# A leftover tile's first-layer sums turned by VectorE and a trip through DRAM instead of by TensorE

## The chip, the cores and the metric

One core of a Trainium2 chip runs the kernel. The metric is the device time of one execution in microseconds (us). Before the change the median of three runs is 629.51 us (629.24 to 629.6). TensorE multiplies matrices, VectorE, ScalarE and GpSimd work elementwise, and SP and ScalarE issue the DMAs of this kernel. In the rows of the profile they are PE (PEld for its weight loads), DVE, ACT, POOL and SP; ACTq and SPq are the sequencers that issue DMAs.

## The reference

Windowed attention feeds a mixture of four experts with fixed weights (the first MLP), and that feeds a second MLP with h * cos(h) between its layers.

```python
def _moe_ref(x, domain_probs, w1, w2):          # x: 1152 x 512, four experts, F = 1024
    p = domain_probs / (domain_probs.sum(-1, keepdims=True) + 1e-09)
    for e in range(E):
        h = np.maximum(x @ w1[e], 0.0)
        out += p[:, e:e + 1] * (h @ w2[e])

def _moe2_ref(x, w_in, w_out):                  # 512 -> 2048 -> 512
    h = x @ w_in
    g = h * np.cos(h)
    return g @ w_out
```

## The kernel before

The 1152 tokens are nine tiles of 128: eight that are worked on as two blocks of 512 columns, and one leftover, tile 0. Every float32 product is three matmuls, over a first part in a shorter form (fp32r) and the rest (`PASSES`). The hidden columns are worked on in twelve groups of 512: groups 0 to 7 are the first MLP (`g < NG1`), 8 to 11 the second. A group has two phases.

In the products phase the eight tiles' first layer is computed by a scheme that needs seven products instead of eight. `pair(g, j)` (line 835) does one half of the group's columns: seven products of six matmuls each, into four PSUM banks `pa`, `pb`, `pc`, `pd`. VectorE forms sums between them: `u1 = pb + p1`, `c22 = pc + u1`, `c22 += pd`. The sixth product adds into `pc` and the seventh into `pd`, so they can't start before VectorE has read those banks for `c22`. In the second MLP (`early == 2`) the order is pa, pb, again pa, pc, pd, then the sixth (on pc) and the seventh (on pd). `finish` (line 753) makes the hidden values: Relu in the first MLP, a cosine chain in the second. `cosine` (line 704) is ScalarE read and round, a VectorE subtract (line 713), ScalarE sine, a VectorE multiply (line 722); `cosine_parts` splits the result in a first part (ScalarE) and a second part (GpSimd).

In the layer 2 phase, nine tiles of twelve matmuls each (`layer2`, line 937) go to `acc`. Tile 0 is placed where `"0"` or 0 stands. Somewhere in it `left(g + 1)` ("La", "Lb", line 795) computes the leftover's first layer of the next group, twelve matmuls, with tokens in the rows of PSUM. The second layer needs them with hidden columns in the rows: `turn_rows` ("X", line 821) transposes the four 128x128 blocks on TensorE, and ScalarE and VectorE split them into `h0`. In the first MLP Relu comes ahead of that (line 810), in the second the cosine (`cosine_rows`, line 734).

The order of the work is written by hand. `steps` (line 1020) lists each group's steps, and `run` (line 1096) does for each: the step's matmuls, `stages` advances of the open cosine chains, `njobs` pieces of weight preparation for the next group (a ScalarE copy and a GpSimd subtraction each, with the raw loads on SP), `ncv` pieces of weight conversion (groups 0 to 5: int64 words to float32 by ScalarE and VectorE, through DRAM), and then what follows the step's matmuls. Each engine works in the order of issue. In the second MLP `early_kind` is 2 for groups 9 to 11, and the second piece group of a group's weights (`second`, line 246) is done at the second and third product (`more`).

Group 8 and group 0 have places of their own for the leftover's turn (lines 1035 and 1166).

Of the kernel before, what the change touches and what calls it, by code (L numbers as in the profile page):

```python
# [10 lines left out]
F32 = mybir.dt.float32  # L11
# [4 lines left out]
AF = mybir.ActivationFunctionType  # L16
ALU = mybir.AluOpType
# [15 lines left out]
G = 512  # L33
NFG = G // 128
NG1, NG2 = E * F1 // G, F2 // G
NTT = NT // 128
MAGIC = 12582912.0
INV2PI = 0.15915494309189535
# [14 lines left out]
def tile_kernel(ctx, tc, qT, kT, v, probs, w_1, w_2, w_in, w_out, out):  # L53
    nc = tc.nc
# [3 lines left out]
    dram = pool("dram", bufs=1, space=DRAM)  # L58
# [8 lines left out]
    txp = pool("txp", bufs=4)  # L67
# [114 lines left out]

    wi32 = dram.tile([DM, F2], F32, name="wi32")
    wo32 = dram.tile([F2, DM], F32, name="wo32")

    def sub(eng, out, a, b):
        eng.tensor_tensor(out=out, in0=a, in1=b, op=ALU.subtract)  # L187
# [506 lines left out]
    h0 = hp.tile([128, 2, NFG, 128], F32R, name="h0")  # L694
# [9 lines left out]
    def cosine(ps, out):  # L704

        u = csp.tile([128, NB], F32, name="u", tag="c")
        r = csp.tile([128, NB], F32, name="r", tag="c")

        nc.scalar.activation(out=u, in_=ps, func=AF.Copy, scale=INV2PI, bias=0.25)
        nc.scalar.activation(out=r, in_=u, func=AF.Copy, bias=MAGIC)  # L710
        yield False
        yield False
        nc.vector.scalar_tensor_tensor(  # L713
            out=u, in0=r, scalar=MAGIC, in1=u, op0=ALU.subtract, op1=ALU.subtract
        )
        yield False
        nc.scalar.activation(out=u, in_=u, func=AF.Sin, scale=-TWOPI)
        yield False
        yield False
        if out is None:  # L720
            out = u
        nc.vector.tensor_tensor(out=out, in0=ps, in1=u, op=ALU.mult)
        yield out

    def cosine_parts(ps, hi, lo, eng):

        for u in cosine(ps, None):
            yield False
        nc.scalar.activation(out=hi, in_=u, func=AF.Copy)  # L729
        if eng is nc.vector:  # L730
            yield False
        sub(eng, lo, u, hi.bitcast(F32))

    def cosine_rows(ps, out):

        for _ in cosine(ps, out):
            yield False

    def chain(c, ch):
        next(ch)  # L740
        chains.append((c, ch))
# [48 lines left out]
    def sums():  # L790
        return bank([128, 512], "o_ps")

    rows_t = {}

    def left(g):

        ps = sums()
        for d in range(ND):
            for a, bb in PASSES:
                nc.tensor.matmul(  # L800
                    ps.rearrange("p (j f) -> p j f", j=2), x0[:, bb, d, :],
                    w1[:, :, a, 0, d * 256 : (d + 1) * 256],
                    start=(d == 0 and (a, bb) == PASSES[0]),
                    stop=(d == ND - 1 and (a, bb) == PASSES[-1]),
                )
            if d % 2:
                yield
        r = rows_t[g] = lp.tile([128, 512], F32, name="lt", tag="lt")
        if g < NG1:
            nc.scalar.activation(out=r, in_=ps, func=AF.Relu)  # L810
        else:
            chain(0, cosine_rows(ps, r))

    def half(step, end):

        next(step)
        yield
        if end:
            whole(step)

    def turn_rows(g):

        apart = mm is None
        assert not any(c == 0 for c, _ in chains)
        r = rows_t.pop(g)
        tp = bank([128, NFG, 128], "l_ps")
        for f in range(NFG):
            nc.tensor.transpose(tp[:, f, :], r[:, f * 128 : (f + 1) * 128], ident)  # L828
        yield
        nc.scalar.activation(out=h0[:, 0], in_=tp, func=AF.Copy)  # L830
        if apart:
            yield
        sub(nc.vector, h0[:, 1], tp, h0[:, 0].bitcast(F32))
# [86 lines left out]
    def ahead(g, t):  # L920

        opened[g, t] = sums()
        tile_matmuls(opened[g, t], g, t, range(NFG // 2))
        yield
# [12 lines left out]
    def layer2(g, t, ps=None):  # L937
        if (g, t) == (NG1 + NG2 - 1, LAST):
            yield from last_tile(g, t)
            return  # L940
        f0 = NFG // 2 if (g, t) in opened else 0
        ps = opened.pop((g, t), None) or ps or sums()
        tile_matmuls(ps, g, t, range(f0, NFG))
        yield
        o = acc(t)
        if g < NG1:
            s = pr[:, t, g // 2 : g // 2 + 1]
            if g == 0:
                nc.vector.tensor_scalar(out=o, in0=ps, scalar1=s, scalar2=None, op0=ALU.mult)
            else:  # L950
                nc.vector.scalar_tensor_tensor(  # L951
                    out=o, in0=ps, scalar=s, in1=o, op0=ALU.mult, op1=ALU.add
                )
        elif g == NG1:
            nc.vector.tensor_copy(o, ps)
        else:
            nc.vector.tensor_tensor(out=o, in0=ps, in1=o, op=ALU.add)  # L957
            if g == NG1 + NG2 - 1:
                store(t, o)
# [38 lines left out]
    def bank(shape, name):  # L998
        count[0] += 1
        from_, tag = ps1, "o_ps"  # L1000
        if mm is not None and count[0] % 4:
            from_, tag = mm[0]
            mm.append(mm.pop(0))
        return from_.tile(shape, F32, name=name, tag=tag)
# [15 lines left out]
    def steps(g):  # L1020

        last, turn = g == NG1 + NG2 - 1, g == NG1 - 1
        moe = g < NG1
        early_kind = 1 if g in (0, NG1) else 0 if moe else 2
        ps = [early.pop(j, None) or pair(g, j, early_kind) for j in range(2)]
        if g == 0:
            yield ahead(0, 0), 0, 0, 0
            for p in ps:  # L1030
                next(p)
            seq = [0, 1, 0, 1, 0, 0, 1, 0, "0", 1, 1]
            more = [1, 1, 0, 0, 0, 0, 0, 2, 1, 0, 0]
        elif g == NG1:
            seq = [0, 0, 0, 0, "X", 0, 1, 1, "0", 1, 1, 1]
            more = [0, 1, 1, 0, 0, 0, 0, 0, 0, 0, 0, 0]
        elif moe:
            seq = [0] * 7 + [1] * 7
            more = [0, 1, 1, 0, 0, 0, 0] + [0, 1, 1, 1, 1, 1, 1]
        else:  # L1040
            seq = [0] * 7 + ["0"] + [1] * 7
            more = [0, 1, 1, 0, 0, 0, 0, 0] + ([0] * 7 if last else [0, 1, 1, 0, 0, 0, 0])
        for j, m in zip(seq, more):
            if j == "X":
                yield turn_rows(g), 2, m, 0
            elif j == "0":
                yield layer2(g, 0), 2, m, 0
            else:
                yield ps[j], 1, m, 0
        nxt = None if last else left(g + 1)  # L1050
        ncv = {0: 2, 5: 3, 6: 3, 1: 3, "La": 3, 7: 3, 2: 3, 8: 3}
        if turn:
            order = (0, 1, "f0", 5, "f1", 2, "f5", 6, "f2", 3, "f6", 4, "f3", 7, "f4", 8, "f7")
            njobs = [2, 2, 0, 2, 0, 2]
        elif moe:
            order = (0, 5, 6, 1, "La", "Lb", 7, 2, 8, 3, "X", 4)
            njobs = [1] * 8
            if g == 0:
                order = (5, 6, 1, "La", "Lb", 7, 2, 8, 3, "X", 4)
                njobs[:3] = [2, 2, 2]  # L1060
                ncv = {5: 1, 6: 2, 1: 3, "La": 1, 7: 3, 2: 3, 8: 3}
        elif last:
            order, njobs = ("a5", "a6", "a7", "a8", "a1", 5, 6, 7, 8, 1, 2, 3, 4), []
        else:
            order = ("a5", "a6", "a7", "a8", "a1", "a2", 5, 6, 7, "La", 8, "Lb", 1, 2, 3, "X", 4)
            njobs = [0, 0, 0, 0, 0, 0, 1, 1, 1, 1, 1, 1, 1, 1, 1, 1, 2]
            if g == NG1:
                njobs[4:6] = [1, 1]
        for k, o in enumerate(order):
            m = njobs.pop(0) if njobs else 0  # L1070
            if isinstance(o, int):
                assert o == 0 or not any(c > 0 for c, _ in chains)
                yield layer2(g, o), 2, m, ncv.get(o, 0)
            elif o[0] == "f":
                yield flip(int(o[1])), 0, m, 0
            elif o[0] == "a":
                yield ahead(g, int(o[1])), 2 if last else 1, m, 0
            elif o[0] == "L":
                yield half(nxt, o == "Lb"), 2, m, ncv.get(o, 0)
            else:  # L1080
                yield turn_rows(g + 1), 2, m, 0
        if turn:
            yield from last_flip(g + 1, nxt)
# [24 lines left out]
    with tc.manual_schedule():  # L1108
# [19 lines left out]
        def leftover(end):  # L1128
            if not first:
                first.append(left(0))  # L1130
            return half(first[0], end)
# [146 lines left out]
```

## Time and profile before

| | |
|---|---|
| median of three runs | 629.51 us |
| span of the profiled execution, first to last instruction | 627.9 us |
| between the two (launch and end of a run) | 1.6 us |
| TensorE busy | 621.4 us, 99% |
| VectorE, ScalarE, GpSimd busy | 71%, 52%, 56% |
| granted TensorE clock | 0.999 |

The profiled execution has no time of its own beside its span, so sums are made against the span of 627.9 and carried to the runs by the 1.6 us. A group of the first MLP takes 46.7 us from one first product to the next (342.04 to 388.77), one of the second 46.7 or 46.8 (487.40 to 534.17). Times in the rows are us from the start of the span. A matmul's duration is its length in a pipeline; matmuls start closer together than that.

### The profile page before, as it was taken

The page shows a single profiled execution, that of the slowest core. Times are in us where ns is not written, and L with a number is a line of the kernel's source. Part 1 is how long each engine was busy: PE and PEld are TensorE (multiplying, and loading weights), DVE is VectorE, ACT ScalarE, POOL GpSimd, SP SyncE. Part 2 cuts the span into 40 slices and gives each one's busy share as a digit, 9 for nine tenths or more (in the row PEclk, how much of TensorE's full clock was granted, in tenths as well). Part 3 has the DMA queues.
Part 4 walks back from the last instruction along what each step waited for, and adds up shares of the span by engine and source line. Part 5 has one row for each costly group of instructions (what it writes and reads, how often), then busy time and mean ns, then how long its engine had stood idle before and what let it go on. Part 6 is the DMA issues. An engine that isn't in the chain of part 4 may idle for free.

```text
span 627.9 us, 9396 instructions
## 1 busy us (share of the span) xinstructions
PE 621.4 (99%) x3408; PEld 508.8 (81%) x3408; DVE 445.3 (71%) x776; ACT 324.0 (52%) x690; POOL 350.4 (56%) x338
## 2 busy tenths in 40 slices
PE   8999999999999999999999999999999999999997
PEld 6777888888888788888888888888788888888886
DVE  6878899589788788789689633656774664664663
ACT  6989444435444344344344331455883683673660
POOL 4868495463562482573553561592459479379340
PEclk9999999999999999999999999999999999999999
DMA  9651245147147147146143111120101201202003
GB/s 276 166 155 42 94 123 176 35 153 242 43 135 244 58 140 241 54 147 206 34 164 137 34 68 34 33 89 14 34 1 48 87 2 68 67 1 67 16 2 135
DMA packets 39118, 60.66 MB, mean 97 GB/s; under 512 B 4640, under 2 KB 21536, under 8 KB 39072
## 3 DMA queue, kind: packets, MB, share of 16 engines
q1 hardware_dynamic: 38528, 59.67, 29.6%
q8 instruction: 27, 0.44, 0.3%
q10 hardware_dynamic: 544, 0.39, 0.2%
q14 instruction: 19, 0.16, 0.1%
HBM read 49.30 MB, written 10.75 MB: 96 GB/s over the span
## 4 chain that ended last, share of the span: by engine, by line
PE 92%; DVE 3%; ACT 2%; POOL 1%; issue 1%; DMA 1%; SPq 0%; DVEq 0%; POOLq 0%
PE o_ps L930 46%; PE o_ps L771 33%; PE o_ps L800 5%; PE x_ps L612 2%; PE t_ps L576 1%; PE s_ps L506 1%; PE l_ps L828 1%; DMA wo<-cv 1%; PE r_ps L550 1%; PE o_ps L1114 1%; ACT p L525 1%; PE f_ps L984 1%; PE o_ps L968 0%; POOL w1t L187 0%; ACT r L710 0%
## 5 line engine op out<-in xcount | busy, mean ns | idle before, releaser
L930 PE MATMUL o_ps<-w2t,hpair 128*128 128x512 f32 x1140 | 267.4, 391 | 0.0
L930 PEld LDWEIGHTS o_ps<-w2t,hpair 128*128 128x128 f32 x1140 | 212.7, 188 | 43.8
L771 PE MATMUL o_ps<-xs,w1t 128*128 128x512 f32 x720 | 169.3, 390 | 0.0
L771 PEld LDWEIGHTS o_ps<-xs,w1t 128*128 128x128 f32 x720 | 134.6, 188 | 28.5 <-issue 0.4
L187 POOL TENSOR_TENSOR w2t<-raw,w2t 128x512 fp32r<-128x512 f32 x48 | 64.0, 1349 | 78.6 <-ACT w2t L211 78.4
L187 POOL TENSOR_TENSOR w1t<-raw,w1t 128x512 fp32r<-128x512 f32 x48 | 64.3, 1357 | 61.3 <-ACT w1t L211 60.2
L187 POOL TENSOR_TENSOR w1t<-sm,w1t 128x512 fp32r<-128x512 f32 x48 | 63.8, 1346 | 31.3 <-ACT w1t L211 31.0
L771 PE MATMUL o_ps<-xz,w1t 128*128 128x512 f32 x288 | 69.9, 390 | 0.4 <-DVE c L839 0.4
L187 POOL TENSOR_TENSOR hpair<-u,hpair 128x512 fp32r<-128x512 f32 x30 | 40.1, 1346 | 51.4 <-ACT hpair L729 51.4
L771 PEld LDWEIGHTS o_ps<-xz,w1t 128*128 128x128 f32 x288 | 53.7, 188 | 12.4 <-DVE c L839 1.0
L310 ACT ACTIVATE cr<-cr 128x512 f32<-128x512 f32 x32 | 21.7, 678 | 79.8 <-DVE cv L304 79.8
L951 DVE SCALAR_TENSOR_TENSOR accpair<-o_ps,pr,accpair 128x512 f32<-128x512 f32 x56 | 41.2, 745 | 27.0 <-PE o_ps L930 27.0
L757 ACT ACTIVATE hpair<-o_ps 128x512 fp32r<-128x512 f32 x47 | 28.1, 597 | 35.0 <-DVE o_ps L839 35.0
L748 DVE SCALAR_TENSOR_TENSOR hpair<-o_ps,hpair 128x512 fp32r<-128x512 f32 x47 | 32.3, 688 | 19.2 <-ACT hpair L757 19.1
L211 ACT ACTIVATE w1t<-sm 128x512 fp32r<-128x512 f32 x44 | 27.6, 628 | 31.9 <-POOL sm L187 31.7
L713 DVE SCALAR_TENSOR_TENSOR u<-r,u 128x512 f32<-128x512 f32 x36 | 28.1, 780 | 11.1 <-ACT r L710 11.0
L800 PE MATMUL o_ps<-w1t,x 128*128 128x512 f32 x144 | 35.7, 391 | 0.0
L957 DVE TENSOR_TENSOR accpair<-o_ps,accpair 128x512 f32<-128x512 f32 x23 | 15.7, 689 | 27.9 <-PE o_ps L930 27.9
L839 DVE TENSOR_TENSOR o_ps<-o_ps,u 128x512 f32<-128x512 f32 x48 | 33.3, 693 | 2.9 <-PE o_ps L771 2.6
L930 PE MATMUL o_ps<-w2t,h 128*128 128x512 f32 x144 | 35.2, 391 | 0.1
L304 DVE SCALAR_TENSOR_TENSOR cv<-cr,cv 128x512 int32<-128x512 int32 x32 | 33.6, 1050 | 1.1
L757 ACT ACTIVATE hpair<-c 128x512 fp32r<-128x512 f32 x17 | 10.7, 631 | 45.6 <-DVE c L839 45.6
(137 smaller groups left out, 873.8 us busy)
## 6 DMA issues: line engine op xcount, KB each, us to landing
raw<-w SPq DMA_DIRECT2D x32, 512.0 KB, 3.8
cr<-w_in SPq DMA_DIRECT2D x16, 512.0 KB, 4.3
cr<-w_out SPq DMA_DIRECT2D x16, 512.0 KB, 4.0
wi<-cv SPq DMA_DIRECT2D x16, 256.0 KB, 3.4
wo<-cv SPq DMA_DIRECT2D x16, 256.0 KB, 2.2
raw<-wi SPq DMA_DIRECT2D x8, 512.0 KB, 3.4
raw<-wo SPq DMA_DIRECT2D x8, 512.0 KB, 3.6
qt<-qT SPq DMA_DIRECT2D x8, 256.0 KB, 3.9
```

The lines of the kernel that those rows point to most:

```text
L187: eng.tensor_tensor(out=out, in0=a, in1=b, op=ALU.subtract)
L211: nc.scalar.activation(out=out, in_=src, func=AF.Copy)
L304: nc.vector.scalar_tensor_tensor(out=a, in0=hw, scalar=-0x40000000, in1=o, op0=ALU.bitwise_and, op1=ALU.bitwise_or,)
L310: nc.scalar.activation(out=fl(hw), in_=fl(hw), func=AF.Abs)
L713: nc.vector.scalar_tensor_tensor(out=u, in0=r, scalar=MAGIC, in1=u, op0=ALU.subtract, op1=ALU.subtract)
L748: nc.vector.scalar_tensor_tensor(out=out, in0=src, scalar=0.0, in1=hi.bitcast(F32), op0=ALU.max, op1=ALU.subtract)
L757: nc.scalar.activation(out=hi, in_=src, func=AF.Relu)
L771: nc.tensor.matmul(ps, w(a, k, m), operand_of_x(bb, b)[:, m], start=(start and m == 0 and (a, bb) == PASSES[0]), stop=(stop and m == 1 and ...
L800: nc.tensor.matmul(ps.rearrange("p (j f) -> p j f", j=2), x0[:, bb, d, :], w1[:, :, a, 0, d * 256 : (d + 1) * 256], start=(d == 0 and (a, ...
L839: add = lambda out, a, b: nc.vector.tensor_tensor(out=out, in0=a, in1=b, op=ALU.add)
L930: nc.tensor.matmul(ps, hidden(a, f, t), w_t[2, g, f // 2][:, bb, f % 2, :], start=(f == 0 and (a, bb) == PASSES[0]), stop=(f == NFG - 1 an ...
L951: nc.vector.scalar_tensor_tensor(out=o, in0=ps, scalar=s, in1=o, op0=ALU.mult, op1=ALU.add)
```

## The change

For all groups but 0 and 8 (`shuffled`), VectorE turns the 32x32 squares of the leftover's sums from PSUM into SBUF at the end of `left`. The sixteen squares' places within the 128x128 blocks are put right by DMA: `store_rows` writes them to a DRAM tensor with four stores (two from SP's queue, two from ScalarE's), issued ahead of tile 2 of layer 2, and `load_rows` fetches them with one load on SP, issued ahead of the step behind tile 2. No TensorE transpose remains for these groups. The split into `h0` moves to the next group's products phase: behind the fourth product in the first MLP. In the second MLP the cosine moves too: what is stored are the plain sums, and the cosine chain opens the products phase, advanced twice at each of the first three products. The one job that "X" had in the second MLP's list goes to tile 4.

```diff
-        nc.scalar.activation(out=u, in_=ps, func=AF.Copy, scale=INV2PI, bias=0.25)
+        like = (lambda t: t) if len(ps.shape) == 2 else (lambda t: t.rearrange("p (k t e) -> p k t e", k=NFG, e=32))
+        nc.scalar.activation(out=like(u), in_=ps, func=AF.Copy, scale=INV2PI, bias=0.25)
...
+    def shuffled(g):
+        return g not in (0, NG1)
+
+    def store_rows(g):
+        r = rows_t.pop(g)
+        to = rows32.rearrange("(q e) (t n) -> t e q n", e=32, t=4)
+        for t in range(4):
+            queue = nc.scalar if t % 2 else nc.sync
+            queue.dma_start(out=to[t], in_=r[32 * t : 32 * t + 32].rearrange("e (q n) -> e q n", q=4))
+
+    def load_rows(g):
+        r = rows_t[g] = txp.tile([128, 4, 128], F32, name="lm", tag="x1", bufs=1)
+        nc.sync.dma_start(out=r.rearrange("p t n -> p (t n)"), in_=rows32)
+
+    def shuffled_rows(g):
+        yield
+        src = rows_t.pop(g).rearrange("p t (k e) -> p k t e", e=32)
+        hi, lo = (h0[:, a].rearrange("p k n -> p (k n)") for a in range(2))
+        if g < NG1:
+            hi, lo = (x.rearrange("p (k t e) -> p k t e", k=NFG, e=32) for x in (hi, lo))
+            nc.scalar.activation(out=hi, in_=src, func=AF.Copy)
+            sub(nc.vector, lo, src, hi.bitcast(F32))
+        else:
+            chain(0, cosine_parts(src, hi, lo, nc.gpsimd))
...
         r = rows_t[g] = lp.tile([128, 512], F32, name="lt", tag="lt")
-        if g < NG1:
+        if shuffled(g):
+            if g < NG1:
+                nc.scalar.activation(out=ps, in_=ps, func=AF.Relu)
+            nc.vector.transpose(
+                r.rearrange("p (q k e) -> p q k e", q=4, e=32),
+                ps.rearrange("p (k q e) -> p q k e", q=4, e=32),
+            )
+        elif g < NG1:
...
         elif moe:
-            seq = [0] * 7 + [1] * 7
-            more = [0, 1, 1, 0, 0, 0, 0] + [0, 1, 1, 1, 1, 1, 1]
+            seq = [0] * 4 + ["X"] + [0] * 3 + [1] * 7
+            more = [0, 1, 1, 0, 0, 0, 0, 0] + [0, 1, 1, 1, 1, 1, 1]
         else:
-            seq = [0] * 7 + ["0"] + [1] * 7
-            more = [0, 1, 1, 0, 0, 0, 0, 0] + ([0] * 7 if last else [0, 1, 1, 0, 0, 0, 0])
-        for j, m in zip(seq, more):
+            seq = ["X"] + [0] * 7 + ["0"] + [1] * 7
+            more = [0, 0, 1, 1, 0, 0, 0, 0, 0] + ([0] * 7 if last else [0, 1, 1, 0, 0, 0, 0])
+        for k, (j, m) in enumerate(zip(seq, more)):
             if j == "X":
-                yield turn_rows(g), 2, m, 0
+                yield turn_rows(g), 0 if shuffled(g) else 2, m, 0
...
-                yield ps[j], 1, m, 0
+                yield ps[j], 2 if g > NG1 and k < 4 else 1, m, 0
...
-            order = (0, 5, 6, 1, "La", "Lb", 7, 2, 8, 3, "X", 4)
+            order = (0, 5, 6, 1, "La", "Lb", 7, 2, 8, 3, 4)
...
-            order = ("a5", "a6", "a7", "a8", "a1", "a2", 5, 6, 7, "La", 8, "Lb", 1, 2, 3, "X", 4)
-            njobs = [0, 0, 0, 0, 0, 0, 1, 1, 1, 1, 1, 1, 1, 1, 1, 1, 2]
+            order = ("a5", "a6", "a7", "a8", "a1", "a2", 5, 6, 7, "La", 8, "Lb", 1, 2, 3, 4)
+            njobs = [0, 0, 0, 0, 0, 0, 1, 1, 1, 1, 1, 1, 1, 1, 1, 3]
...
         for k, o in enumerate(order):
             m = njobs.pop(0) if njobs else 0
+            if nxt and shuffled(g + 1):
+                if o == 2:
+                    store_rows(g + 1)
+                if order[k - 1] == 2:
+                    load_rows(g + 1)
```

## Rows read from the trace of the kernel before

**Rows 1.** The page's part 1: busy us, share of the span, instructions.
```profile
span 627.9 us, 9396 instructions
...
PE 621.4 (99%) x3408; PEld 508.8 (81%) x3408; DVE 445.3 (71%) x776; ACT 324.0 (52%) x690; POOL 350.4 (56%) x338
```

**Rows 2.** The page's part 4: the chain that ended last, by engine.
```profile
PE 92%; DVE 3%; ACT 2%; POOL 1%; issue 1%; DMA 1%; SPq 0%; DVEq 0%; POOLq 0%
```

**Rows 3.** Timeline, start of group 10's products: start, us, engine, line, tiles [idle before].
```profile
532.79 2.55 POOL L187 TENSOR_TENSOR w2t<-raw,w2t 128x512 fp32r<-128x512 f32 x2 [0.24 <-ACT w2t L211]
...
534.17 6.96 PE L771 MATMUL o_ps<-xs,w1t 128*128 128x512 f32 x30
534.37 0.69 DVE L957 TENSOR_TENSOR accpair<-o_ps,accpair 128x512 f32<-128x512 f32 x1 [1.45 <-PE o_ps L930]
...
535.73 0.60 ACT L845 ACTIVATE p<-o_ps 128x512 f32<-128x512 f32 x1 [2.50 <-PE o_ps L771]
536.22 1.15 ACT L211 ACTIVATE w2t<-raw 128x512 fp32r<-128x512 f32 x2
536.92 2.54 POOL L187 TENSOR_TENSOR w2t<-raw,w2t 128x512 fp32r<-128x512 f32 x2 [1.58 <-ACT w2t L211]
537.16 0.69 DVE L839 TENSOR_TENSOR u<-o_ps,p 128x512 f32<-128x512 f32 x1 [2.10 <-PE o_ps L771]
538.45 0.60 ACT L709 ACTIVATE u<-o_ps 128x512 f32<-128x512 f32 x1 [1.08 <-PE o_ps L771]
...
539.81 0.69 DVE L839 TENSOR_TENSOR c<-o_ps,u 128x512 f32<-128x512 f32 x1 [1.96 <-PE o_ps L771]
540.42 0.68 DVE L713 SCALAR_TENSOR_TENSOR u<-r,u 128x512 f32<-128x512 f32 x1
...
540.97 2.88 PE L771 MATMUL o_ps<-xz,w1t 128*128 128x512 f32 x12
541.17 0.69 DVE L839 TENSOR_TENSOR c<-o_ps,c 128x512 f32<-128x512 f32 x1
```

**Rows 4.** Groups of instructions, shapes apart: count, busy us, mean ns, idle before.
```profile
L828 PE MATMUL l_ps<-ident,lt 128*128 128x128 f32 x48 | 7.2, 273 | 0.0
...
L955 DVE COPY accpair<-o_ps 128x512 f32<-128x512 f32 x8 | 5.4, 688 | 10.1 <-PE o_ps L930 10.1
```

**Rows 5.** Timeline of TensorE around one turn of the leftover, group 5.
```profile
338.85 0.60 PE L828 MATMUL l_ps<-ident,lt 128*128 128x128 f32 x4
339.21 2.99 PE L930 MATMUL o_ps<-w2t,hpair 128*128 128x512 f32 x12
342.04 6.96 PE L771 MATMUL o_ps<-xs,w1t 128*128 128x512 f32 x30
```

**Rows 6.** Timeline, group 10: GpSimd and VectorE at the same time.
```profile
547.13 1.30 POOL L187 TENSOR_TENSOR hpair<-u,hpair 128x512 fp32r<-128x512 f32 x1 [7.67 <-ACT hpair L729]
547.32 1.65 DVE L722 TENSOR_TENSOR u<-c,u 128x512 f32<-128x512 f32 x1
```

**Rows 7.** Timeline of ScalarE at the start: its queue issues two DMAs.
```profile
0.73 0.99 ACTq L168 DMA_DIRECT2D k<-kT  x2
```

**Rows 8.** Timeline, group 9: TensorE behind the leftover's last matmul.
```profile
525.52 5.61 PE L930 MATMUL o_ps<-w2t,hpair 128*128 128x512 f32 x24
```

**Rows 9.** DMA issues: count, KB each, median us from issue to landing.
```profile
vt<-v SPq DMA_DIRECT2D x8, 256.0 KB, 4.8
...
kt<-kT SPq DMA_DIRECT2D x3, 256.0 KB, 3.4
...
out<-acc SPq DMA_DIRECT2D x2, 128.0 KB, 2.3
```

**Rows 10.** Timeline of VectorE in the second pair of group 6.
```profile
355.84 0.69 DVE L839 TENSOR_TENSOR c<-o_ps,u 128x512 f32<-128x512 f32 x1 [0.60 <-PE o_ps L771]
```

**Rows 11.** Timeline of VectorE, then of TensorE, at group 3's products.
```profile
202.55 0.43 DVE L300 TENSOR_SCALAR cv<-cr 128x512 int32<-128x512 int32 x1 [1.81 <-DMA wo<-cv]
...
208.55 3.02 PE L771 MATMUL o_ps<-xz,w1t 128*128 128x512 f32 x12 [0.40 <-DVE c L839]
```

More of the change, by code (lines that the diff above doesn't have):

```diff
@@ L184, in tile_kernel @@
     wo32 = dram.tile([F2, DM], F32, name="wo32")
+    rows32 = dram.tile([128, G], F32, name="rows32")
     def sub(eng, out, a, b):
@@ L721, in cosine @@
             out = u
-        nc.vector.tensor_tensor(out=out, in0=ps, in1=u, op=ALU.mult)
+        nc.vector.tensor_tensor(out=like(out), in0=ps, in1=like(u), op=ALU.mult)
         yield out
@@ L821, in turn_rows @@
     def turn_rows(g):
+        if shuffled(g):
+            yield from shuffled_rows(g)
+            return
         apart = mm is None
@@ L1055, in steps @@
         elif moe:
-            order = (0, 5, 6, 1, "La", "Lb", 7, 2, 8, 3, "X", 4)
+            order = (0, 5, 6, 1, "La", "Lb", 7, 2, 8, 3, 4)
             njobs = [1] * 8
             if g == 0:
-                order = (5, 6, 1, "La", "Lb", 7, 2, 8, 3, "X", 4)
+                order = (5, 6, 1, "La", "Lb", 7, 2, 8, 3, 4)
                 njobs[:3] = [2, 2, 2]
```

## The prediction

> **What bounds the kernel now.** I read the page's busy table first, then TensorE's timeline around the step that goes, then the timeline of all engines in a second-MLP group, because the change adds its work there. TensorE is busy 99% of the span [rows 1], and the chain that ended last is 92% TensorE [rows 2]. So a matmul taken out is a gain, and any other engine matters only where TensorE has to wait for it. The reader should see how little waiting there is: 30 product matmuls take 6.80 us, from 534.17 to 540.97 [rows 3], so six take 1.36 and twelve 2.72.
>
> **The transposes that go.** Groups 1 to 7 and 9 to 11 lose four TensorE transposes each. The table of groups gives 273 ns for one [rows 4], which would make 40 x 0.273 = 10.9 us. That is a length in the pipeline, not a spacing. The block starts at 338.85, the next matmul at 339.21, and the next product at 342.04 [rows 5]: 3.19 us for the four transposes and twelve matmuls, and the twelve alone take 2.72. The step costs TensorE 0.47 us, so ten cost 4.7 us. It stands on the path, as TensorE waits for nothing before or behind it. This term is a gain for sure: **-4.7 us**.
>
> **What is added off TensorE.** VectorE turns 32x32 blocks out of PSUM. No row shows that operation. The nearest is the copy of the same size out of PSUM, 0.69 us [rows 4]; I take it, with 0.60 (ScalarE's read of a product, [rows 3]) and 1.65 (the longest VectorE row quoted, [rows 6]) as ends. The first MLP's Relu stays, in place. Then come four stores of 64 KB, two issued by SP and two by ScalarE, and a fetch of 256 KB on SP. Two issues on ScalarE's queue took 0.99 us [rows 7]. ScalarE's two issues wait for VectorE's turn, and what is queued behind them is weight copies that TensorE needs a group later; SP's fetch waits for the four landings, with raw weight loads (and, in groups 0 to 5, conversion traffic) behind it. I cost these queues at nothing on the path because the weights are a group ahead; the price if that cover is gone is the third rival.
>
> When does the fetch land? In groups 8 to 10 the leftover's last matmul ends at 525.52 in the group shown [rows 8]. Turn ends +0.9, the second issue is out at +1.3, a small store takes 2.3 [rows 9], so the fetch goes at about +3.7; 256 KB take 3.4 to 4.8 [rows 9], so it lands at +7.1 to +8.5. Between lie the rest of tile 1 and tile 2 (six matmuls each) and tiles 3 and 4 (twelve each): 1.36 + 1.36 + 2.72 + 2.72 = 8.16. It lands at about the first product of the next group, which I call P.
>
> **First MLP (groups 1 to 7).** The split of the leftover's hidden values moves between the products: one ScalarE operation (about 0.6) and one VectorE operation (0.69) after the fourth product. There VectorE is late by little: VectorE idles 0.60 us before the next pair's second sum at 355.84 [rows 10], so the shift is taken up. What wants care is the conversion groups. In group 3 TensorE already waits 0.40 us for VectorE's c sum, after VectorE waited 1.81 us for a conversion store to land [rows 11]. The turn adds 0.69 in front of that, the old subtraction (as long) goes behind it. So between -0.4 (the wait vanishes) and +0.7 (one turn's length added to it); I take **+0.15**.
>
> **Second MLP (groups 9 to 11), where I expect the gain to go.** The cosine of the leftover (read, round, VectorE subtract, sine, VectorE multiply, ScalarE first part, GpSimd second part) moves from the tiles of layer 2 to the first three products. Here is the order that the code gives, from P on, with times of [rows 3]. ScalarE operations of this size follow each other by 0.53 (two in 1.15), VectorE's by 0.61, GpSimd's by 1.27.
> - VectorE adds the last tile at +0.20, then the subtract of the cosine. GpSimd's two weight parts of layer 2 end at 535.34, P + 1.17, and P comes 0.47 earlier, so the subtract is done by +2.2 at the latest. ScalarE copies p1 at +1.56; the sine follows at +2.05 (+2.2 at the latest; what follows takes the early value), then the weight copy at +2.57 (it stood at +2.05). GpSimd's weight part begins at +3.27 and holds to +4.56.
> - VectorE's u1 sum is tied to TensorE at +2.99; the multiply is behind it, ready at +3.6. Both its inputs are in SBUF. A row shows what that costs: GpSimd works from 547.13 to 548.43, the same form of multiply starts at 547.32 and ends at 548.97 [rows 6], 0.54 after GpSimd. So it ends at +5.10 here.
> - ScalarE's first part +5.14, the second weight copy +5.67, and only then the read of product A, +6.19 (it stood at +4.28: 538.45), its rounding done at +7.44.
> - VectorE's subtract of that chain is queued ahead of the sum c += pd. GpSimd meanwhile does the leftover's second part (+5.84) and the second weight part (+7.09 to +8.38), so the subtract, ready at +7.48, ends at +8.92, and the sum at +9.55. It stood at 541.17, +7.00 [rows 3].
> - The seventh product adds into the bank that this sum reads, and is due at P + 8.16. It starts at +9.6: TensorE waits 1.44 us, plus about 0.1 for restarting (as behind the transposes, where twelve matmuls last 2.99 against 2.88 [rows 3, 5]): **1.55 us** in each of three groups, **+4.65**.
>
> Before, the margin at this place was 8.16 - 7.69 = 0.47 us. After the stall the chain is late by some 0.3 us against TensorE, which the next pair takes up.
>
> The Trainium skill (SBUF - State Buffer, Who interferes with whom) says that a VectorE instruction with two SBUF inputs fully blocks against a GpSimd one that reads SBUF, and that one with at most one SBUF input, outside the two-port modes, doesn't contend. The pair in [rows 6] agrees. By that rule the turns, which read PSUM, are exempt; if they were not, each could take up to 1.65, which the range holds.
>
> **Sum.** 627.9 (span) - 4.7 + 0.15 + 4.65 = 628.0. The runs' median lies 1.6 above the profiled span (629.51 against 627.9), so **629.6 us**: no change.
>
> **Rivals.** *A, the collision is half as bad or missing.* If GpSimd's weight part starts 0.35 us later than I placed it (0.15 of that is open above), so that the multiply gets the port first, the multiply ends at +4.28, the read of A starts at +5.36, and the subtract is ready at +6.66. If only that one meets GpSimd it ends near +8.1, the sum near +8.7, the wait is 0.65: -4.7 + 0.15 + 2.0 = 627.0. If neither does, 625.0. For it: a margin of 0.3 us between GpSimd's start and the multiply decides. Against: GpSimd has three parts back to back, and two tries to miss them.
> *B, the turn isn't what costs, and 10.9 us go.* The 273 ns would have to be a spacing; the next matmul starts 0.36 us after the first of four [rows 5]. 618.6 us, hardly.
> *C, the trip through DRAM is late.* ScalarE then stands at the cosine's first read with p1, the weight copies and A's read behind it, and TensorE waits for the sum of the fourth product as well. Up to about P + 2 the wait stays near 1.5, since the pieces then miss each other by other amounts. From there each us costs about one: a landing at P + 4 puts the multiply at +6.4, the first c sum at +7.05 against a product due at +6.80, the second at about +11: some 3.3 us a group, 9.9 in all, 634.9 us. For it: store and fetch cannot overlap, and raw weights of 512 KB share the queues. Against: by the rows it lands at about P, so it would need 2 us more than the slowest.
> The Trainium skill (VectorE: DVE Perf Modes, Rules for kernel authors) advises TensorE for 128x128 transposes whose result may go to PSUM, which is the old way; by that rule the new one loses, and C, or the collision above, is how it would do so here.
>
> **How the numbers follow.** This kernel's measurement can tell about 0.2%, 1.26 us, from no change; so "same" is 628.25 to 630.77. My forecast 0.42. Rival A 0.38 (625.0 to 628.2). B 0.01. C, and conversion groups losing more than 0.7 us, 0.19 (630.8 to 635). So faster 0.39, same 0.42, slower 0.19. The range leaves out one in ten at each end: 625.0 to 632.2; for the likeliest case alone it is 628.3 to 630.7.
>
> **What would show it.** Right: no transposes of l_ps in groups 1 to 7 and 9 to 11; the first MLP's seven groups each about 0.47 us shorter; in groups 9, 10 and 11 a gap on TensorE of 1 to 1.7 us ahead of the seventh product, put down to VectorE's c sum, and a multiply of about 1.5 us. Wrong: no gap there (A), or ScalarE idle at the cosine's first read until a DMA (C); VectorE turns far from 0.7 us; TensorE waiting for h0 at the leftover's tile; or gaps in groups 1 to 5, where conversion work is squeezed.

## The result, and the profile after

| | before | after |
|---|---|---|
| median | 629.38 us (629.22 to 629.6, 4 runs) | 633.88 us (633.35 to 635.06, 4 runs) |
| ratio after to before | | 1.0076, interval 1.0061 to 1.0091 |
| span of the profiled execution | 627.9 us | 633.1 us |
| TensorE busy | 621.4 us, 99% | 620.2 us, 98% |

The kernel became slower by 0.8%; I had said no change, 629.6 us, with 632.2 as the upper end. The page of after, part 1 (busy us, share, instructions) and the first line of part 4 (the chain that ended last), against [rows 1, 2]:

```profile
span 633.1 us, 9421 instructions
...
PE 620.2 (98%) x3368; PEld 505.9 (80%) x3368; DVE 453.8 (72%) x783; ACT 325.0 (51%) x690; POOL 352.7 (56%) x341
...
PE 87%; DVE 4%; ACT 3%; DMA 2%; issue 2%; POOL 1%; SPq 0%; DVEq 0%; POOLq 0%
```

TensorE has 40 instructions fewer, yet the chain is 87% TensorE instead of 92%: VectorE, ScalarE and DMAs have a larger part in it. To see where, I took the time from each group's first product to the next one's (the last group: to the last matmul). It is worked out from the start times of all product matmuls:

| group | 0 | 1 | 2 | 3 | 4 | 5 | 6 | 7 | 8 | 9 | 10 | 11 |
|---|---|---|---|---|---|---|---|---|---|---|---|---|
| before | 70.39 | 46.70 | 46.74 | 47.40 | 46.73 | 46.71 | 46.73 | 47.23 | 51.40 | 46.77 | 46.74 | 43.57 |
| after | 69.91 | 46.24 | 46.24 | 51.48 | 46.24 | 46.24 | 46.24 | 47.24 | 50.94 | 47.66 | 48.07 | 45.15 |

Seven groups lost 0.46 to 0.50 us: the transposes sit in the layer 2 phase of groups 0 to 6 and 8 to 10, one group ahead of their use. Group 3 gained 4.08, and groups 9, 10 and 11 gained 0.89, 1.33 and 1.58. With the 0.47 that groups 3, 9 and 10 also saved, group 3 lost 4.55 to waiting and the second MLP 4.74. Together -4.7 + 4.55 + 4.74 = 4.6 us; the median rose by 4.5. The span of the profiled execution rose by 5.2. This one was the longest of the four runs (635.06 us), and 0.5 of the 5.2 lies ahead of the first product, which starts between 36.7 and 38.3 us in the profiles of this document.

**Group 5, no transposes.** Timeline of TensorE in after where [rows 5] stood: layer 2 goes straight on to the next group's products.

```profile
337.84 6.51 PE L971 MATMUL o_ps<-w2t,hpair 128*128 128x512 f32 x28
344.18 1.07 PE L773 MATMUL o_ps<-xs,w1t 128*128 128x512 f32 x4
```

**Group 10, the forecast collision.** Timeline of all engines in after, from 536.26 = P on, answering to [rows 3]; the first line is ScalarE's first read of the fetched sums:

```profile
534.74 0.63 ACT L711 ACTIVATE u<-lm 128x512 f32<-128x512 f32 x1 [0.68 <-DMA lm<-rows]
...
539.54 1.28 POOL L188 TENSOR_TENSOR w2t<-raw,w2t 128x512 fp32r<-128x512 f32 x1 [2.18 <-ACT w2t L212]
539.86 1.51 DVE L724 TENSOR_TENSOR u<-lm,u 128x512 f32<-128x512 f32 x1
...
542.46 0.58 ACT L711 ACTIVATE u<-o_ps 128x512 f32<-128x512 f32 x1
...
543.37 1.29 POOL L188 TENSOR_TENSOR w2t<-raw,w2t 128x512 fp32r<-128x512 f32 x1
543.74 1.48 DVE L715 SCALAR_TENSOR_TENSOR u<-r,u 128x512 f32<-128x512 f32 x1 [1.14 <-ACT r L712]
545.13 0.68 DVE L880 TENSOR_TENSOR c<-o_ps,c 128x512 f32<-128x512 f32 x1
...
545.87 1.66 PE L773 MATMUL o_ps<-xz,w1t 128*128 128x512 f32 x6 [1.29 <-DVE c L880]
```

The leftover's multiply takes 1.51 us beside GpSimd instead of 0.69, the read of product A comes at P + 6.20, its subtract takes 1.48 beside GpSimd again, and the sum ends at P + 9.55. The seventh product should have started at P + 8.16 and starts at P + 9.61.

**Group 3, not forecast.** Timeline of GpSimd and VectorE in after at group 3's products (P = 200.22), then that of TensorE, answering to [rows 11]. `cv` are the tiles of the weight conversion:

```profile
202.98 2.72 POOL L188 TENSOR_TENSOR w2t<-raw,w2t 128x512 fp32r<-128x512 f32 x2 [4.61 <-ACT w2t L212]
203.33 1.23 DVE L301 TENSOR_SCALAR cv<-cr 128x512 int32<-128x512 int32 x1 [1.86 <-DMA wo<-cv]
204.59 1.66 DVE L305 SCALAR_TENSOR_TENSOR cv<-cr,cv 128x512 int32<-128x512 int32 x1
...
206.99 2.06 DVE L992 SCALAR_TENSOR_TENSOR accpair<-o_ps,pr,accpair 128x512 f32<-128x512 f32 x3
208.97 0.68 DVE L880 TENSOR_TENSOR u<-o_ps,p 128x512 f32<-128x512 f32 x1
209.75 0.69 DVE L880 TENSOR_TENSOR c<-o_ps,u 128x512 f32<-128x512 f32 x1
```

```profile
200.22 6.96 PE L773 MATMUL o_ps<-xs,w1t 128*128 128x512 f32 x30
210.50 4.61 PE L773 MATMUL o_ps<-xz,w1t 128*128 128x512 f32 x12 [3.31 <-DVE c L880]
```

A conversion store's landing frees VectorE's first conversion operation at P + 3.11; before it was P + 1.35 (202.55 against a first product at 201.20). GpSimd's weight parts have begun by then, so two conversion operations take 1.23 and 1.66 us where they took 0.43 and 0.69. Behind them on VectorE stand three accumulations and the sums, and the sixth product starts at 210.50 instead of P + 6.80 = 207.02: 3.48 us late. (Waits here are counted by start times; the idle time in the rows, 3.31, counts from the modelled end of the matmul before.) Then the twelve matmuls take 4.61 us instead of 2.88. The windows of after around it (busy time and count of PE, PEld, DVE, ACT, POOL; then granted clock, DMA share, GB/s) show why:

```profile
207.00:211.00 4.00, 0.69 (x3) 0.46 (x3) 3.79 (x7) 0.00 (x0) 0.00 (x0) 1.00 0.35 121
211.00:215.00 4.00, 4.00 (x12) 3.13 (x12) 2.74 (x5) 2.16 (x4) 0.00 (x0) 0.57 0.00 0
215.00:219.00 4.00, 4.00 (x19) 3.30 (x18) 2.68 (x4) 2.19 (x5) 0.89 (x1) 1.00 0.00 0
```

The granted clock is 0.57 over these four microseconds, and matmuls start 0.427 us apart instead of 0.227: the lower of the two levels, 1.2 instead of 2.4 GHz. Eight matmuls at 0.2 us more make 1.6 us. So 3.48 of wait, 0.1 for restarting and 1.6 of slow work make up group 3's excess over 46.24 in this profile, which is 5.24.

### The profile page after: what moved, and what is told of

It is laid out like the page before. It is cut to its first block, busy times and chain, and to the rows that moved or that the text cites. A ratio compares the mean times of both kernels' runs of the same rounds, so it can differ in the third digit from the quotient of the medians.

```text
span 633.1 us, 9421 instructions
## 1 busy us (share of the span) xinstructions
PE 620.2 (98%) x3368; PEld 505.9 (80%) x3368; DVE 453.8 (72%) x783; ACT 325.0 (51%) x690; POOL 352.7 (56%) x341
## 4 chain that ended last, share of the span: by engine, by line
PE 87%; DVE 4%; ACT 3%; DMA 2%; issue 2%; POOL 1%; SPq 0%; DVEq 0%; POOLq 0%
PE o_ps L971 45%; PE o_ps L773 30%; PE o_ps L831 5%; PE x_ps L613 2%; PE t_ps L577 1%; PE s_ps L507 1%; ACT r L712 1%; DMA rows<-lt 1%; DMA wo<-cv 1%; ACT u L711 1%; PE r_ps L551 1%; DVE c L880 1%; DVE u L724 1%; PE o_ps L1160 1%; PE f_ps L1025 1%
## 5 line engine op out<-in xcount | busy, mean ns | idle before, releaser
L188 POOL TENSOR_TENSOR w1t<-sm,w1t 128x512 fp32r<-128x512 f32 x48 | 63.8, 1344 | 31.9 <-ACT w1t L212 31.6
L773 PE MATMUL o_ps<-xz,w1t 128*128 128x512 f32 x288 | 72.4, 399 | 6.6 <-DVE c L880 6.6
L715 DVE SCALAR_TENSOR_TENSOR u<-r,u 128x512 f32<-128x512 f32 x36 | 30.6, 850 | 10.9 <-ACT r L712 10.9
L301 DVE TENSOR_SCALAR cv<-cr 128x512 int32<-128x512 int32 x32 | 31.1, 972 | 3.8 <-DMA wi<-cv 2.0
```

The source lines that it names most:

```text
L301: nc.vector.tensor_scalar(out=o, in0=hw, scalar1=3, scalar2=0x3FFFFFF8, op0=ALU.logical_shift_left, op1=ALU.bitwise_and,)
L715: nc.vector.scalar_tensor_tensor(out=u, in0=r, scalar=MAGIC, in1=u, op0=ALU.subtract, op1=ALU.subtract)
L773: nc.tensor.matmul(ps, w(a, k, m), operand_of_x(bb, b)[:, m], start=(start and m == 0 and (a, bb) == PASSES[0]), stop=(stop and m == 1 and ...
```

## The experiments

Two questions stood after the result. For groups 9 to 11: the collision of the forecast, against a late fetch (rival C). For group 3: its own trip makes the conversion store late, against TensorE merely coming there sooner because of the transposes that went. The medians of before that go with the experiments are 630.13 (e1 to e4), 629.29 (e5 to e7, e9) and 629.02 us (e8), so ratios are compared. After has 1.0076.

**e1, the first MLP's part alone**

```diff
-        return g not in (0, NG1)
+        return 0 < g < NG1
```

The second MLP's list of steps is the old one.

> Only groups 1 to 7 turn by VectorE and DMA; groups 9 to 11 keep TensorE's transposes and the cosine in layer 2. Theory (the loss sits at two separate places): the seven turns save 7 x 0.47 = 3.3 us and group 3's products lose 4.56 against before (3.48 instead of 0.55 of waiting, and 1.7 us at half clock behind it), so the time is about 629.4 - 3.3 + 4.6 = 630.7 us and the second MLP's groups last as before. Rival (the added DMA traffic slows everything a little): the loss is spread, no one group is longer by more than 1 us, and the time is near 632.

630.57 us, ratio 1.0015 (1.0004 to 1.0027). Groups 9 to 11 take 46.76, 46.73 and 43.57, as before; group 3 takes 51.28. Timeline of e1 at group 3 (first product at 199.28):

```profile
202.15 1.46 DVE L301 TENSOR_SCALAR cv<-cr 128x512 int32<-128x512 int32 x1 [1.62 <-DMA wo<-cv]
...
209.56 4.43 PE L773 MATMUL o_ps<-xz,w1t 128*128 128x512 f32 x12 [3.32 <-DVE c L880]
```

The first MLP's half saves seven times 0.47 = 3.3 us and loses more than that in the one group.

**e2, the second MLP's part alone**

```diff
-        return g not in (0, NG1)
+        return g > NG1
```

The first MLP's lists of steps are the old ones.

> Only groups 9 to 11 turn by VectorE and DMA; the first MLP is as before. Theory: the three turns save 1.4 us, and groups 9, 10 and 11 lose 1.2, 1.8 and 1.6 us by TensorE's wait ahead of the seventh product and its small successors, so about 629.4 - 1.4 + 4.6 = 632.6 us, with group 3 as before (0.55 us of waiting). Rival (the waits of the second MLP come from being shifted against the raw weight loads by what happens in group 3): the waits are smaller than 0.5 us and the time is 628.0.

633.64 us, ratio 1.0068 (1.0048 to 1.0089), a us more than I expected. Group 3 is at 47.35 (47.40 before); groups 9, 10 and 11 take 48.07, 48.06 and 45.16, and in each TensorE waits ahead of the seventh product, 1.67 us from matmul to matmul, so 1.45 more than the spacing and about 0.1 for restarting. Timeline of e2, group 10 (P = 534.37), the seventh product:

```profile
543.97 1.66 PE L773 MATMUL o_ps<-xz,w1t 128*128 128x512 f32 x6 [1.28 <-DVE c L880]
```

The two losses are independent: e1's 0.15% and e2's 0.68% add up to after's 0.76% within the intervals.

**e3, the sum ahead of the cosine's subtract**

```diff
-        at_once = j and g >= NG1
+        at_once = g > NG1 or (j and g >= NG1)
```

`add(c22, pd, c22)` is issued before the step's cosine stages instead of behind them. The multiply still meets GpSimd; only the order on VectorE changes.

> The changed kernel with one line altered: in groups 9 to 11 VectorE does the sum c += pd of the first half ahead of the waiting subtract of product A's cosine, not behind it. Theory (TensorE waits because this sum is queued behind a subtract that waits for ScalarE and for GpSimd's port): the sum is done at P + 7.7, ahead of the seventh product's 8.16, the three waits (0.96, 1.56, 1.56) go, and the time is 633.9 - 4.1 = 629.8 us. Rival (the cosine chains as a whole are late, so the wait moves on to the second parts of the hidden values, at the tiles of layer 2): the gap ahead of the seventh product goes but TensorE waits as long for GpSimd's second parts, and the time stays above 632.5.

629.79 us, ratio 0.9999 (0.9989 to 1.0008). Timeline of e3, group 10 (P = 535.38):

```profile
538.66 1.28 POOL L188 TENSOR_TENSOR w2t<-raw,w2t 128x512 fp32r<-128x512 f32 x1 [2.24 <-ACT w2t L212]
538.98 1.51 DVE L724 TENSOR_TENSOR u<-lm,u 128x512 f32<-128x512 f32 x1
...
542.18 2.88 PE L773 MATMUL o_ps<-xz,w1t 128*128 128x512 f32 x12
...
542.38 0.69 DVE L880 TENSOR_TENSOR c<-o_ps,c 128x512 f32<-128x512 f32 x1 [0.67 <-PE o_ps L773]
...
542.99 1.35 DVE L715 SCALAR_TENSOR_TENSOR u<-r,u 128x512 f32<-128x512 f32 x1
```

Both collisions are still there (1.51 and 1.35), and TensorE runs its twelve matmuls without a wait: the sum reads PSUM, is done at P + 7.69, and the seventh product finds its bank free. Groups 9 to 11 take 46.29, 46.40 and 43.56. So the loss needs the sum's place on VectorE behind the slowed chain; the collisions alone cost TensorE nothing. Group 3 still took 50.96 here, and group 4 47.84.

**e9, the weight pieces out of the way**

```diff
-            more = [0, 0, 1, 1, 0, 0, 0, 0, 0] + ([0] * 7 if last else [0, 1, 1, 0, 0, 0, 0])
+            more = [0, 0, 0, 0, 1, 1, 0, 0, 0] + ([0] * 7 if last else [0, 1, 1, 0, 0, 0, 0])
```

> The changed kernel with the two weight pieces in the products of groups 9 to 11 done at the fourth and fifth product, not the second and third. Theory (the wait ahead of the seventh product comes from ScalarE's weight copies and GpSimd's weight parts in the way of the leftover's cosine): the multiply takes about 0.7 and not 1.5 us, the read of A comes by P + 5, the subtract is done ahead of c += pd's turn, and the waits (0.96, 1.56, 1.56 us) shrink to under 0.3 each: 633.9 - 3.5 = 630.4 us or below. Rival (the cosine's own seven operations are too much for the first products, whatever else is there): the waits stay above 1 us and the time at 633 to 634.

629.25 us, ratio 1.000 (0.999 to 1.001). Timeline of e9, group 10 (P = 534.59), the multiply:

```profile
538.18 0.68 DVE L724 TENSOR_TENSOR u<-lm,u 128x512 f32<-128x512 f32 x1
```

The multiply is 0.68 at the same P + 3.59 where it was 1.51, and groups 9 to 11 take 46.24, 46.24 and 43.55. The edit moves ScalarE's weight copies along with GpSimd's parts: the read of product A comes 1.35 us sooner, at P + 4.85, of which 0.83 is the multiply and the rest a copy that no longer stands ahead of it. So the two weight pieces in the chain's way were the cause, and moving them or moving the sum mends the same loss. In this kernel's profile group 3 lost less than in after, and group 4 lost as well (48.05 and 49.06).

**e4, the last conversion step of a group left out of its place**

```diff
-        ncv = {0: 2, 5: 3, 6: 3, 1: 3, "La": 3, 7: 3, 2: 3, 8: 3}
+        ncv = {0: 2, 5: 3, 6: 3, 1: 3, "La": 3, 7: 3, 2: 3}
```

The three conversion pieces behind tile 8 move to later steps, so none reaches into the products.

> The changed kernel with the three conversion pieces at tile 8 taken out of each group of the first MLP from 1 on (20 pieces a group instead of 23; they are done later, up to group 6, the work is the same). Theory (group 3 loses because VectorE's conversion work at the end of a group runs into its products): no conversion work is left within 5 us of the first product, group 3 waits for nothing, its half-clock spell goes too, and the time is 633.9 - 4.6 - 0.7 = 628.6 us. Rival (the trip through DRAM and its queues make group 3 late): the stores, the fetch and their waits are all still there, so group 3 still loses over 3 us and the time is above 632.

628.97 us, ratio 0.9985 (0.9974 to 0.9996). Groups 3 and 4 take 46.24 each, with the granted clock at 1.0 throughout. Timeline of e4, group 3 (P = 200.65), the sixth and seventh product:

```profile
207.45 2.88 PE L773 MATMUL o_ps<-xz,w1t 128*128 128x512 f32 x12
```

Without the conversion on VectorE there is no wait in group 3, although the whole trip is still there. In group 9 this run shows rival A: timeline of e4 (P = 483.77), then of after (P = 488.60), at the subtract of product A:

```profile
490.49 0.69 DVE L715 SCALAR_TENSOR_TENSOR u<-r,u 128x512 f32<-128x512 f32 x1 [0.39 <-ACT r L712]
490.50 1.84 POOL L188 TENSOR_TENSOR w2t<-raw,w2t 128x512 fp32r<-128x512 f32 x1
```

```profile
495.26 1.86 DVE L715 SCALAR_TENSOR_TENSOR u<-r,u 128x512 f32<-128x512 f32 x1 [0.16 <-ACT r L712]
495.27 1.30 POOL L188 TENSOR_TENSOR w2t<-raw,w2t 128x512 fp32r<-128x512 f32 x1
```

VectorE and GpSimd start within 0.01 us of each other in both. In e4 VectorE has 0.69 and GpSimd 1.84, and the group loses 0.27 (46.51); in after VectorE has 1.86 and TensorE waits 0.96 us with its restart. Which engine goes first decides about 1 us. In group 9 of both, the multiply itself got ahead of GpSimd's part.

**e6, the same edit to the kernel before**

> The kernel before, without the conversion pieces at tile 8: a control for what that line brings alone. Theory: only group 3's wait of 0.67 us (0.55 and its restart) goes, ratio near 0.999, about 0.6 to 0.7 us. Rival (conversion work slowed other places too, so the line is worth more than the changed kernel shows): over 1.5 us.

628.71 us, ratio 0.9993 (0.9984 to 1.0002). Group 3 falls from 47.40 to 46.70, which is its wait of [rows 11], and nothing else moves. So before had no more than these 0.7 us open to it; the rest of e4's repair takes away what the change had made worse.

**e7, group 3's leftover turned by TensorE, all others by VectorE**

```diff
-        return g not in (0, NG1)
+        return g not in (0, 3, NG1)
```

with the old list of steps where group 3's leftover is made and used.

> The changed kernel, but the leftover of group 3 is turned by TensorE as before (groups 1, 2, 4 to 7 and 9 to 11 by VectorE and DMA). It tells apart why group 3 loses 4.56 us. Theory E (TensorE is early: it reaches group 3 about 0.5 us sooner, with its weight parts on GpSimd sooner too, where they hold the port against VectorE's conversion pieces): the wait is still 1.5 us or more in group 3 although nothing of its own trip is left. Theory D (the group's own turn, two issues on ScalarE and the stores delay the conversion store that VectorE waits for): the wait is back near 0.55 to 1.1 us, and the time is near 633.9 - 4.2 = 629.7 us.

630.22 us, ratio 1.0017 (1.0007 to 1.0028). The products of group 3 start 162.89 us behind those of group 0, against 163.83 in before and 162.39 in after: e7 keeps group 2's transposes, so TensorE has two of its three gains of 0.47. (Times from the start of the span can't be compared here, as group 0 starts up to 1.5 us apart in them.) TensorE waits for nothing. Timeline of e7, VectorE and TensorE at group 3 (P = 200.20):

```profile
200.86 0.43 DVE L301 TENSOR_SCALAR cv<-cr 128x512 int32<-128x512 int32 x1 [1.70 <-DMA wo<-cv]
201.32 0.69 DVE L305 SCALAR_TENSOR_TENSOR cv<-cr,cv 128x512 int32<-128x512 int32 x1
...
207.00 2.89 PE L773 MATMUL o_ps<-xz,w1t 128*128 128x512 f32 x12
```

So coming 0.94 us early makes no wait without group 3's own trip; e8 has all three gains and shows that they make none either. The store lands at P + 0.66, and both conversion operations are through before GpSimd's parts begin at P + 2.76.

**e8, all four stores of a trip issued by SP**

```diff
-            queue = nc.scalar if t % 2 else nc.sync
-            queue.dma_start(out=to[t], in_=r[32 * t : 32 * t + 32].rearrange("e (q n) -> e q n", q=4))
+            nc.sync.dma_start(out=to[t], in_=r[32 * t : 32 * t + 32].rearrange("e (q n) -> e q n", q=4))
```

> All four stores of each trip are issued by SP, none by ScalarE; the rest is the changed kernel. If ScalarE's two issues (0.84 us) are what makes group 3's conversion store late: its weight copy there, and with it GpSimd's part, SP's raw load and the conversion store behind that, come some 0.7 us earlier, the landing comes at about the first product + 2.3 us instead of + 3.1, at least the first conversion operation is done before GpSimd's weight parts begin, and TensorE's wait ahead of the sixth product is 2 us or less instead of 3.5, without the stretch at half clock; groups 3 and 4 together 95 us or less instead of 97.7, ratio to before about 1.003. Rival, the issues don't matter (the turn's own place on VectorE and the traffic of the trip set it): wait 3 to 3.7 us, half clock, ratio 1.0065 to 1.009. The waits of groups 9 to 11 (1.1 to 1.7 us) stay under both.

629.18 us, ratio 1.0003 (0.9984 to 1.0022). Group 3 takes 46.27 and group 4 46.48, and the first product of group 3 comes 162.39 us behind that of group 0, as in after; the waits of groups 9 to 11 are as in after. Timelines around the trip in the layer 2 phase ahead of group 3: e8 (P = 200.63) first, then after (P = 200.22):

```profile
194.40 0.70 DVE L842 STREAM_TRANSPOSE lt<-o_ps 128x512 f32<-128x512 f32 x1
...
195.08 0.63 ACT L212 ACTIVATE w2t<-raw 128x512 fp32r<-128x512 f32 x1
195.13 1.77 SPq L806 DMA_DIRECT2D rows<-lt  x4
...
197.66 0.39 SPq L318 DMA_DIRECT2D wo<-cv  x1
...
201.92 0.43 DVE L301 TENSOR_SCALAR cv<-cr 128x512 int32<-128x512 int32 x1 [0.48 <-DMA wo<-cv]
```

```profile
194.74 0.70 DVE L843 STREAM_TRANSPOSE lt<-o_ps 128x512 f32<-128x512 f32 x1
...
195.46 0.80 SPq L807 DMA_DIRECT2D rows<-lt  x2
195.47 0.84 ACTq L807 DMA_DIRECT2D rows<-lt  x2
...
196.36 0.63 ACT L212 ACTIVATE w2t<-raw 128x512 fp32r<-128x512 f32 x1 [0.85 <-DVE cv L309]
...
197.07 1.29 POOL L188 TENSOR_TENSOR w2t<-raw,w2t 128x512 fp32r<-128x512 f32 x1 [2.81 <-ACT w2t L212]
...
198.39 0.40 SPq L204 DMA_DIRECT2D raw<-w  x1
198.88 0.46 SPq L318 DMA_DIRECT2D wo<-cv  x1
```

In after ScalarE's weight copy stands behind two issues, which themselves stand behind VectorE's turn (195.44). The profile puts its idle 0.85 down to VectorE, but the queue's two issues, 0.84, fill that stretch. It starts at P - 3.86; in e8, free of them, at P - 5.55. GpSimd's part of that weight waits for the copy, SP's raw load for the part's buffer, and the conversion store is queued behind the raw load on SP: P - 1.34 in after, P - 2.97 in e8. It lands at P + 3.11 and P + 1.29.

Not all of that is the issues': the turn itself starts 0.75 us earlier against P in e8 (P - 6.23 against P - 5.48). Counted from the turn's start the copy comes after 1.62 us in after and 0.68 in e8, so the issues are worth 0.94. e9 has both issues and its turn at P - 6.06, nearly as early as e8's. Timeline of e9 (P = 200.53), the copy:

```profile
196.09 0.63 ACT L212 ACTIVATE w2t<-raw 128x512 fp32r<-128x512 f32 x1 [0.83 <-DVE cv L309]
```

That is P - 4.44, e9's store lands at P + 2.20, and TensorE still waits 1.67 us in group 3. So the two issues, passed on through GpSimd and SP, decide between a wait and none, and where the turn falls decides how long it is. The single runs bear this out. A stretch of 3.4 us at half clock lowers the mean granted clock of a run to about 0.997, as in the profiles of after, e1 and e3. It is 0.997 or less in 31 of the 34 runs of after, e1, e3 and e9, in one of ten of e8, and in none of before, e2, e4, e5, e6 and e7.

**e5, both repairs** (the edits of e3 and e4 together)

> The changed kernel with both one-line alterations: c += pd ahead of the waiting subtract in groups 9 to 11, and no conversion pieces at tile 8. Theory (two independent places, their gains add): against the kernel before, 10 x 0.47 = 4.7 us of transposes and group 3's old wait of 0.67 go and nothing comes, so 5.4 us, a ratio near 0.9915 (624.0 to 624.8 us). Rival (what is taken from one place comes up at the next one that is tight, as group 4 lost 1.6 us when only the sum was moved): less than 4 us are gained, ratio above 0.994.

624.61 us (624.29 to 625.11), ratio 0.9925 (0.991 to 0.994): faster than both kernels. Groups 1 to 6 take 46.24 each, groups 9 to 11 46.27, 46.40 and 43.55, and the granted clock is 1.0. Timeline of e5, group 3 (P = 199.28), the sixth and seventh product:

```profile
206.08 2.88 PE L773 MATMUL o_ps<-xz,w1t 128*128 128x512 f32 x12
```

The groups of this profile add up to 5.3 us less than in before: ten times 0.47, and the 0.7 of group 3's old wait that e6 takes off too. The medians differ by 4.7 us (3.8 to 5.7 by the interval), and by 4.1 from e6, which shares the line on the conversion.

## Why the prediction was wrong, point by point

**What bounds the kernel: right.** TensorE's matmuls and its waits account for the change within a few tenths of a us.

**Transposes, -4.7: right.** 0.46 to 0.50 in each group against 0.47, and e5 keeps all ten. Rival B is out.

**VectorE's turn, 0.69 taken, 0.60 to 1.65 as ends: right.** The row of after in the groups of instructions (count, busy us, mean ns, idle before):

```profile
L843 DVE STREAM_TRANSPOSE lt<-o_ps 128x512 f32<-128x512 f32 x10 | 7.1, 712 | 5.5 <-ACT o_ps L842 3.5 <-PE o_ps L831 2.0
```

Seven of the ten run while GpSimd works, and none takes more than 0.72. That agrees with the rule of the Trainium skill (SBUF - State Buffer, Who interferes with whom) by which a VectorE instruction with at most one SBUF input, outside the two-port modes, doesn't contend.

**The fetch, landing at about P: right for the second MLP, P - 1.5 to P + 0.9.** For group 10 it went out at 532.11 and ScalarE read it at 534.74, P - 1.52; for group 9 at 489.48, P + 0.88. In groups 1 to 6, for which I had worked out no time, it landed at P + 3.3 to P + 5.3, and its first reader on ScalarE came at P + 6.9 or later, so it cost nothing. The issue-to-landing medians:

```profile
lm<-rows SPq DMA_DIRECT2D x10, 256.0 KB, 3.2
rows<-lt ACTq DMA_DIRECT2D x20, 64.0 KB, 2.5
rows<-lt SPq DMA_DIRECT2D x20, 64.0 KB, 3.3
```

Rival C, near 634.9, is close to the measured time but not its cause: that needed a landing at P + 4, and e3 and e9 remove the loss and leave the trip as it is.

**Second MLP, +4.65: right in mechanism, 4.74, with some luck in the total.** In groups 10 and 11 the wait ahead of the seventh product, with its restart, was 1.555 (forecast 1.55), and the chain behind it fits step by step: multiply end P + 5.11 (5.10), read of A P + 6.20 (6.19), subtract ready P + 7.48 (7.48), sum end P + 9.55 (9.55). In group 9 the fetch came later, the multiply slipped past GpSimd, and only the subtract collided: 0.96, where rival A had said 0.65. The three make 4.07. The rest are small waits that I had not forecast, about 0.2 each: at group 9's third product, and some 31.6 us behind P in groups 9 and 10, where layer 2 waits for a second part from GpSimd. That they fill what group 9 fell short of is luck.

**Group 3, +0.15 with bounds -0.4 and +0.7: this step failed. It measured +4.55.** Four things were wrong in it:
- I costed ScalarE's two issues at nothing on the path "because the weights are a group ahead". For the weights that holds. But SP's raw loads wait for the buffers that the weight parts free, and the conversion store is behind them on SP: the two issues put the copy that frees the buffer back by 0.94 (e8). The price of lost cover that I gave (rival C) was for the fetch, not for this.
- I took the delay to pass on at its own size: one turn's length, 0.69. The landing came 1.76 later against TensorE (P + 3.11 and P + 1.35), and two conversion operations then met GpSimd and took 2.89 us instead of 1.12. [rows 6] had that price; I used it in the second MLP and not here. From 1.76 later and 1.77 longer, 0.60 goes off for the subtraction that moved behind the fourth product: 2.93 for the sum, which started at P + 9.53 instead of P + 6.61 ([rows 11] show its wait). That is the wait of 3.48 against 0.55.
- I said TensorE's own gain counts 0.47 a group. Up to the products of group 3 it is TensorE that gains, three times 0.47, while a chain tied to DMAs and VectorE need not. e8, with the whole gain, shows that this alone costs nothing here: its store lands at P + 1.29, and TensorE doesn't wait.
- A fall of the granted clock behind the wait, 1.6 us in the profile, was not in my sum.

How late the store lands against GpSimd's parts (P + 2.76) orders all the profiles that keep the conversion there, so a threshold lies there, and I had treated it as a slope:

| kernel | first conversion operation at | its two durations | sum c starts at |
|---|---|---|---|
| e7 | P + 0.66 | 0.43, 0.69 | P + 5.92 |
| e2 | P + 1.26 | 0.43, 0.69 | P + 6.52 |
| e8 | P + 1.29 | 0.43, 0.69 | P + 5.96 |
| before | P + 1.35 | 0.43, 0.69 | P + 6.61 |
| e9 | P + 2.20 | 0.43, 0.69 | P + 7.74 |
| e3 | P + 2.52 | 0.43, 1.66 | P + 9.02 |
| e1 | P + 2.87 | 1.46, 1.66 | P + 9.53 |
| after | P + 3.11 | 1.23, 1.66 | P + 9.53 |

(In e3 and e9 the third operation meets GpSimd too, 1.56. Before and e2 have the subtraction of 0.60 still in front.)

**The range and the chances.** "Conversion groups losing more than 0.7" stood in rival C's 0.19, and "gaps in groups 1 to 5" in what would prove me wrong; I gave the two mishaps one small chance and no price of their own. With group 3 at its measured +4.55 my sum gives 628.0 + 4.4 = 632.4 for the span and 634.0 for the median, against 633.88. So close a fit is partly luck: my 1.6 us set a median against one profiled span, while in the runs a time lies 1.8 to 2.3 us above its own span (after's profiled one: 635.06 against 633.1). Rival B's 618.6 leaves out the 0.15 and 4.65 that stand in the sum; with them it is 623.4.

**What stays open.** After, e1, e3 and e9 have the same code up to group 3, and their stores land up to 0.9 us apart in the profiled executions. About 0.6 of that lies ahead of the trip: the turn starts at P - 5.48 in after and e1 and at P - 6.07 in e3 and e9; why is not settled. Nor is it settled what the fall of the clock is worth to a run: after's one run without it took 633.58 us, no less than the others (633.35 to 635.06). Where group 3 waits less, group 4 can lose instead: the two together take 97.1 (e9), 97.6 (e1), 97.7 (after) and 98.8 us (e3) against 92.5 in e4 and e5. e9's profile is the one of its ten runs with a mean clock of 1.0; the others have 0.996 or 0.997, so its groups 3 and 4 may not stand for them. e7's runs are 0.9 us above before, though the groups of its profile add up to 0.3 less. Why e8's runs spread (627.93 to 633.41) where e5's don't isn't either; the slowest of them is the only one with a mean clock of 0.997.

## What to carry to other kernels

An operation that moves to another queue must be followed through everything behind it there, including who waits for the buffers that this frees: here two DMA issues on ScalarE delayed a store on SP, three hand-overs later, by about 0.9 us. Where a delayed operation can slip behind a long neighbour on a shared port, cost it as a threshold: look up when the neighbour starts, and price both sides. A consumer's sum that another engine needs goes ahead of chain work on its in-order queue; this and fewer pieces in the tight place turned +0.8% into -0.75%.

## What the runs showed of the hardware that I had not expected

The granted clock fell to the 1.2 GHz level for 3.4 us (0.57 over four) behind a wait of 3.5 us, 0.8 us after TensorE had taken up work again, and that wait so cost 5.2 in the profile. In e1 the fall came behind a wait as long, at 209.19, 0.4 us ahead of the next matmul. A window of e3 shows the same behind its wait of 3.0 us in group 3 (granted clock third from the right, 0.57):

```profile
210.00:214.00 4.00, 4.00 (x12) 3.14 (x11) 2.68 (x5) 2.23 (x4) 0.00 (x0) 0.57 0.00 0
```

Integer operations of the conversion (SBUF to SBUF) stretch beside GpSimd as the multiply does: 0.43 to 1.23 and 0.69 to 1.66 us. And two starts 0.01 us apart can go either way (e4 and after, group 9). With the same code there, group 9 took 46.51 (e4), 47.61 (e7), 47.66 (after), 47.67 (e8) and 48.07 us (e2).
